# Gated linear attention and a two-level mixture of experts on one core: keys turned head by head, new costs in the planner, 26 of 48 masks on VectorE instead of 21

## The chip, the cores and the metric

The kernel runs on one core of a Trainium2 chip. The core has five engines that run side by side, each through its own list of instructions in order: TensorE (PE in the rows; its weight loads are PEld), VectorE (DVE), ScalarE (ACT), GpSimd (POOL) and SyncE (SP, which here only issues transfers). Sixteen DMA engines move the data. The metric is device time in microseconds (us), lower is better. The kernel before took 367.25 us (median of 3 runs, 365.06 to 367.86).

## The reference, cut to what matters

```
# attention: B=4 batches, H=8 heads, S=768 steps, D=48 wide, all float32
for t in range(S):
    state = alpha[:, :, t, :, None] * state + einsum('bhd,bhe->bhde', k[:, :, t], v[:, :, t])
    y[:, :, t] = einsum('bhd,bhde->bhe', q[:, :, t], state)
x = y.transpose(0, 2, 1, 3).reshape(3072, 384)          # B*S tokens, H*D wide
# mixture of experts: 4 groups of 4 experts, one expert per token, F=1024
g_logits = x @ w_group; g_idx = argmax; g_w = softmax at g_idx
e_logits = x[g] @ w_expert[g]; e_idx = argmax; e_w = softmax at e_idx
out[token] = g_w * e_w * (relu(x @ w1[g, e]) @ w2[g, e])
```

## The kernel before, in words

**Attention.** The 768 steps of a batch are cut into 6 chunks of 128 steps, which makes 24 chunks, numbered 0 to 23; three batches end with chunks 5, 11 and 17, the last with 23. The heads lie in pairs on the partitions: head 2p on rows 0 to 47, head 2p+1 on rows 64 to 111. For each chunk, in the order in which data moves on:

- SyncE loads the chunk (`load`, L486: 962.5 KB with decays, keys, queries and values). Six homes in SBUF are used in turn, and four chunks borrow the homes of the experts' weights. Between the loads of chunks 8 and 12 four transfers fill the experts' slots with zeros (`fill`, L838, 1372 KB each).
- VectorE makes products of the decays with two scans: `back` (L494, backwards), a reciprocal (L500), `forth` (L505).
- GpSimd multiplies them into the keys (`keys`, L510) and the queries (`queries`, L514).
- TensorE makes the scores (`scores`, L528), in two banks, `zs0` and `zs1`, one for each head of a pair; turns the keys (`turned_keys`, L557: four transposes, each of a pair of heads, 112 rows by 128 columns in, 112 columns of identity streamed); makes the key-value products (`gains`, L570), the own outputs from masked scores (`outputs`, L594), the outputs from the state before (`from_before`, L603), and turns the finished rows back (`to_rows`, L617), which gives the routing logits too.
- A mask is due on each of the two score banks. Either VectorE makes it with one multiplication (`mask_all`, L537), or ScalarE copies the bank (`mask_copy`, L542) and GpSimd cuts the copy (`mask_cut`, L545). The table `BY_VECTOR` (L814) says for each chunk how many of the two VectorE takes.
- ScalarE copies the turned keys (`kept_keys`, L562) and the outputs (`copied`, L609), scales the state (`scaled`, L583); VectorE adds the gain to it (`grown`, L579). Chunks 5, 11, 17 and 23 need no turned keys and no gain.

When the logits of a group of chunks are there (6 chunks each in batches 0 to 2; 3, 2 and 1 chunks in the last), VectorE chooses each token's expert in a row of some 13 small operations (L683 to L722), TensorE counts (`counts`, L791), VectorE turns the counts into places, and GpSimd sends the rows of each chunk to their expert's slots (`scatter`, L769, 24 in all).

**Early expert work.** While the last chunks finish, TensorE already computes 96 rows of expert 0 (`add_hidden`, `add_result`, L306) out of batches 0 and 1. After the last scatter has landed, SyncE and ScalarE fetch the rows of the expert that is ahead in count (`fetch_fixed`, L823), VectorE transposes them (`columns_fixed`, L831), and the first full expert can start.

**Experts.** Some 228 us of matrix products follow, expert by expert (`seven`, L1222).

**What sets the order.** For all of the attention, a planner in the kernel's own code (`Plan`, L28) writes the order of every engine's list before anything runs. Each step has an engine, an assumed time `us`, and the steps it comes after; `LAG` is the assumed time from one engine's end to another's start. `order` (L52) takes, again and again, the engine that can start soonest and on it the ready step with the longest way still ahead. A random spread of up to 0.5 us each way, drawn from `seed`, breaks the balance between near equals. TensorE's steps, SyncE's transfers and the scatters are each chained in a fixed sequence of their own (`row=`), so the planner moves freely only the steps of VectorE, ScalarE and GpSimd. At run time each list is kept strictly: a step that waits holds up whatever stands behind it on its engine.

The first eight transfers are issued by SyncE and ScalarE in turn (`begin`, L874).

Of the kernel before, what the change touches and what calls it, by code (L numbers as in the profile page):

```python
# [23 lines left out]
P = 128  # L24
# [3 lines left out]
class Plan:  # L28

    LAG = {ENG.PE: 0.2, ENG.DVE: 0.1, ENG.Activation: 0.2, ENG.Pool: 0.12, ENG.SP: 0.1}  # L30
# [4 lines left out]
    def add(self, name, eng, us, fn, after=(), row=None, lands=0.0, lead=0.0,  # L35
# [8 lines left out]
        return name  # L44

# [6 lines left out]
    def order(self, patience, seed=0, spread=0.0):  # L52
# [28 lines left out]
        while len(done) < len(ops):  # L81
# [12 lines left out]
            free[e] = start + ops[n]["us"]  # L94
            at[n] = start
            done.append(n)
            for m in nexts[n]:
                early[m] = max(early[m], free[e] + self.edge(n, m))
                waits[m] -= 1
                if not waits[m]:  # L100
                    ready[ops[m]["eng"]].append(m)
# [9 lines left out]
def gla_then_hierarchical_moe(  # L111
# [292 lines left out]
    with ExitStack() as gla:  # L404
# [149 lines left out]
        def turned_keys(c):  # L554
            c.zt = output_banks(chunks[max(c.n - 1, 0)])[:, :, 2 * P:2 * P + 2 * R]
            for p in range(HP):
                nc.tensor.transpose(c.zt[:, p // 2, p % 2 * R:(p % 2 + 1) * R], c.k[:, p, :],  # L557
                                    ident[0:R, 0:R])

        def kept_keys(c):  # L560
            c.kt = work.tile([P, HP * R], F32, name="kt")
            nc.scalar.copy(out=c.kt.rearrange("s (b r) -> s b r", b=2), in_=c.zt)  # L562

        def gains(c):
            z = bank()
            for p in range(HP):
                for i in range(2):
                    h = 2 * p + i
                    r = slice(64 * i, 64 if i == 0 else R)
                    nc.tensor.matmul(z[r, p * D:(p + 1) * D],  # L570
                                     lhsT=c.kt[:, p * R + r.start:p * R + r.stop],
# [242 lines left out]
        BY_VECTOR = [1, 0, 0, 1, 1, 2, 0, 0, 0, 1, 1, 2, 1, 1, 1, 0, 0, 2, 2, 1, 0, 2, 0, 2]  # L814
# [51 lines left out]
        L = 400.0  # L866
# [5 lines left out]
        add("first_byte", SP, 1.9, lambda: None, row="sp")  # L872

        def begin(name, by_act, n, a=0, b=IW):  # L874
            add(name, SP, (b - a) * P * 4 / 383.0 / 1e3,
                partial(load, chunks[n], a, b, nc.scalar if by_act else nc.sync),
                row="sp", lands=0.3)
# [3 lines left out]
        begin("decay0", False, 0, 0, HW)  # L881
        begin("decay_0", True, 0, HW, AW)
        begin("key_0", False, 0, AW, KQ)
        begin("query_0", True, 0, KQ, VW)
        begin("decay1", False, 1, 0, AW)
        begin("key_1", True, 1, AW, KQ)
        begin("query_1", False, 1, KQ, VW)
        begin("decay2", True, 2, 0, AW)
# [86 lines left out]
        def add_turned(n):  # L975
# [3 lines left out]
            PEQ(f"turn_k{n}", 0.52, partial(turned_keys, c),  # L979
                after=["ident", late(n - 2, "copy"), late(n - 1, "kept")]  # L980
                + ends_of(n, "key", c.back))
            add(f"kept{n}", ACT, 0.54, partial(kept_keys, c),
# [737 lines left out]
```

## Time and profile before

| what | value |
|---|---|
| median of 3 runs | 367.25 us (365.06 to 367.86) |
| the profiled execution | 367.92 us, of which the span of the trace is 366.2 us |
| TensorE busy in the span | 353.6 us (97%) |
| VectorE busy | 293.1 us (80%) |
| GpSimd busy | 212.8 us (58%) |
| ScalarE busy | 182.0 us (50%) |
| attention with the early expert work | 0 to 128.5 us |
| experts | 128.5 to 356 us |
| last deliveries | 356 to 366.2 us |
| DMA | 98.87 MB, mean 270 GB/s |

Busy shares over the whole span say little here: the kernel is a chain of stages, and which engine or transfer ends last differs from stage to stage. The chain of waits, read from the last instruction back, says what each stretch hangs on, and the timeline of one engine with its idle times says how much room it had. Matmul ends in the trace are modelled, so the start of the next block is the better measure of how long a block took.

### The profile page before, as it was taken

What the parts mean: (1) busy time and instruction counts of PE and PEld (TensorE: products, weight loads), DVE (VectorE), ACT (ScalarE), POOL (GpSimd) and SP (SyncE); (2) the same over time, 40 slices, a digit from 0 to 9 for tenths busy, and PEclk for the clock granted to TensorE, in tenths of its full rate; (3) what the DMA queues carried; (4) which work ended last, traced back from release to release, by engine and by line L of the source; (5) the groups of instructions that cost most, each with busy time, mean ns of one, the idle gap of its engine ahead of it and who ended that gap; (6) DMA issues with size and microseconds to landing.
All of it is one profiled execution on the core that took longest, in us unless ns stands there. A gap on an engine that the chain in (4) does not pass through costs nothing.

```text
span 366.2 us, 16766 instructions
## 1 busy us (share of the span) xinstructions
PE 353.6 (97%) x6890; PEld 331.6 (91%) x6890; DVE 293.1 (80%) x660; ACT 182.0 (50%) x523; POOL 212.8 (58%) x240
## 2 busy tenths in 40 slices
PE   7899999999999999999999999999999999999994
PEld 5688877888888999999999999999999999999994
DVE  6789679999977878989898998988988988895010
ACT  2566755685664142534544445454554454453340
POOL 6898948999986221353544646446354444454544
PEclk9999999999999999999999999999999999999999
DMA  7999997878989599988878878878988988788101
GB/s 271 386 405 384 373 400 287 304 249 300 370 281 401 142 348 238 305 325 235 238 256 231 257 255 254 270 220 286 268 234 281 269 250 302 257 276 274 60 20 35
DMA packets 42461, 98.87 MB, mean 270 GB/s; under 512 B 18853, under 2 KB 23075, under 8 KB 42384
## 3 DMA queue, kind: packets, MB, share of 16 engines
q1 hardware_dynamic: 36496, 87.14, 72.2%
q0 software_dynamic: 4832, 9.55, 7.4%
q8 instruction: 55, 0.90, 1.0%
q10 hardware_dynamic: 1056, 1.10, 0.9%
q14 instruction: 22, 0.18, 0.1%
HBM read 82.61 MB, written 15.60 MB: 268 GB/s over the span
## 4 chain that ended last, share of the span: by engine, by line
PE 80%; DMA 6%; POOL 5%; DVE 4%; issue 3%; ACT 1%; POOLq 0%; SPq 0%; DVEq 0%
PE bank L1222 55%; PE bank L306 5%; DMA ws<-in_rows_dram 5%; PE bank L617 4%; PE zs L528 4%; PE zo L594 3%; PE zs L306 3%; PE zo L603 2%; PE bank L570 2%; PE zo L557 2%; DMA in<-in_rows_dram 2%; DVE kd L494 1%; POOL ws L514 1%; POOL sm L545 1%; DVE ws L287 1%
## 5 line engine op out<-in xcount | busy, mean ns | idle before, releaser
L1370 POOL DMA_INDIRECT out_dram<-yq,dst_q x101 | 109.4, 1083 | 129.3 <-ACT yq L1368 100.9
L1222 PE MATMUL bank<-ts,ws 128*64 128x108 f32 (+13 forms) x1344 | 64.2, 247 | 0.3 <-issue 0.3
L1222 PEld LDWEIGHTS bank<-ts,ws 128*64 128x64 f32 x1344 | 60.2, 137 | 1.0 <-issue 0.4
L1222 PE MATMUL bank<-hT,w 128*64 128x108 f32 (+27 forms) x896 | 58.7, 288 | 0.1
L1222 PEld LDWEIGHTS bank<-hT,w 128*64 128x64 f32 x896 | 50.7, 137 | 4.3 <-ACT hT L1259 0.3
L1222 PE MATMUL bank<-xt_e,w 128*64 128x106 f32 (+12 forms) x1040 | 50.3, 247 | 0.0
L1222 PEld LDWEIGHTS bank<-xt_e,w 128*64 128x64 f32 x1040 | 46.0, 137 | 0.0
L1259 ACT ACTIVATE hT<-hT 128x432 f32<-128x432 f32 (+13 forms) x56 | 29.1, 530 | 21.8 <-DVE hT L1288 15.9
L287 DVE TENSOR_TENSOR ws<-w 128x512 f32<-128x512 f32 x56 | 38.3, 684 | 0.0
L1222 PE MATMUL bank<-ts,w 128*64 128x108 f32 (+13 forms) x672 | 33.2, 247 | 0.0
L1368 ACT ACTIVATE yq<-yq,xq 128x96 f32<-128x96 f32 x91 | 33.0, 373 | 0.3 <-DMA out_dram<-yq,dst_q 0.3
L1222 PEld LDWEIGHTS bank<-ts,w 128*64 128x64 f32 x672 | 30.1, 137 | 0.0
L1363 DVE STREAM_TRANSPOSE yq<-yT 128x672 f32<-128x672 f32 (+2 forms) x16 | 12.9, 809 | 19.8 <-ACT yT L332 12.6
L771 POOL DMA_INDIRECT slots_d<-xr,place x24 | 24.1, 1005 | 5.7 <-issue 4.1
L617 PE MATMUL bank<-wr,yt 112*64 112x116 f32 x384 | 25.4, 267 | 1.0 <-DVE sums L579 0.7
L617 PEld LDWEIGHTS bank<-wr,yt 112*64 112x64 f32 x384 | 20.3, 137 | 1.7 <-issue 0.8
L1326 ACT COPY yT<-bank 128x216 f32<-128x216 f32 (+13 forms) x14 | 4.5, 323 | 34.7 <-PE bank L1222 34.7
L583 ACT ACTIVATE state<-sums,kd 112x48 f32<-112x48 f32 x64 | 17.9, 331 | 6.9 <-DVE sums L579 6.2
L542 ACT COPY sm<-zs 128x512 f32<-128x512 f32 x27 | 15.5, 588 | 10.2 <-PE zs L528 8.9
L609 ACT COPY yt<-zo 112x512 f32<-112x512 f32 x24 | 14.0, 582 | 12.5 <-PE zo L603 10.4
L287 DVE TENSOR_TENSOR ws<-ws,w 128x512 f32<-128x512 f32 x28 | 19.4, 692 | 1.0
L287 DVE TENSOR_TENSOR ws<-w,ws 128x512 f32<-128x512 f32 x28 | 18.7, 668 | 0.0
(221 smaller groups left out, 712.7 us busy)
## 6 DMA issues: line engine op xcount, KB each, us to landing
w<-in_w_dram SPq DMA_DIRECT2D x84, 512.0 KB
ws<-in_rows_dram SPq DMA_DIRECT2D x11, 962.5 KB
w<-in_w_dram SPq DMA_DIRECT2D x6, 1536.0 KB
in<-in_rows_dram SPq DMA_DIRECT2D x6, 962.5 KB
slots_d<-blank SPq DMA_DIRECT2D x4, 1372.0 KB
w<-in_rows_dram SPq DMA_DIRECT2D x4, 962.5 KB
xq<-slots_d SPq DMA_DIRECT2D x28, 85.8 KB
xq<-slots_d SPq DMA_DIRECT2D x28, 73.5 KB
```

Of the source, the lines that this page charges most:

```text
L287: nc.vector.tensor_tensor(out=out, in0=in0, in1=in1, op=op)
L306: nc.tensor.matmul(z, lhsT=w, rhs=x, start=first, stop=last, skip_group_check=True)
L528: nc.tensor.matmul(c.zs[i][s, p, :], lhsT=c.k[r, p, s], rhs=c.q[r, p, :], start=True, stop=True)
L542: nc.scalar.copy(out=c.sm[:, i], in_=c.zs[i])
L583: nc.scalar.activation(out=c.st[:, p, 0:D], in_=chunks[c.n - 1].sums[:, p], func=AF.Copy, scale=c.kd[:, p, 0:1])
L609: nc.scalar.copy(out=c.yt.rearrange("r (a b) s -> r b a s", b=2), in_=c.zo[0:R, :, 0:2 * P].rearrange("r b (a s) -> r b a s", a=2))
L617: nc.tensor.matmul(z[s, p * W:(p + 1) * W], lhsT=c.yt[:, p, s], rhs=wr[:, p, :], start=True, stop=True)
L771: sent = nc.gpsimd.indirect_dma_start(out=slots_by[t], out_offset=bass.IndirectOffsetOnAxis(ap=m["place"][:, c:c + 1], axis=0), in_=xr[:, ...
L1222: nc.tensor.matmul(z[h], lhsT=w[:, h], rhs=x, start=start, stop=False, skip_group_check=True)
L1259: A.activation(out=c, in_=c if z is None else z, func=AF.Relu)
L1368: nc.scalar.activation(out=yq[:, b, :], in_=yq[:, b, :], func=AF.Copy, scale=rows[:, b, QW - 2:QW - 1])
L1370: nc.gpsimd.indirect_dma_start(out=out_by.popleft().rearrange("n (j w) -> (n j) w", j=4), out_offset=bass.IndirectOffsetOnAxis(ap=dst[:, b ...
```

## The change

Five things change. (1) The planner's costs: `LAG` for VectorE and ScalarE are smaller, a step now blocks its engine for a little less than its results take (`OVER`, `held`), some steps' times and the assumed bandwidth `L` are new, and the seed is another. (2) The keys are turned with eight transposes of one head each, on rows 0 to 47 and 64 to 111 by turns, with 48 columns streamed each; the two heads of a pair write to two different banks. (3) The copy of the turned keys is 384 columns wide and not 448, and `gains` reads its weights where they now lie. (4) Among the first transfers, the decays of chunk 1 (now by ScalarE) and the queries of chunk 0 (now by SyncE) swap places. (5) `BY_VECTOR` gives VectorE 7, 2, 6 and 11 masks in batches 0 to 3, and before 5, 4, 6 and 6.

```diff
-    LAG = {ENG.PE: 0.2, ENG.DVE: 0.1, ENG.Activation: 0.2, ENG.Pool: 0.12, ENG.SP: 0.1}
+    LAG = {ENG.PE: 0.2, ENG.DVE: 0.08, ENG.Activation: 0.1, ENG.Pool: 0.12, ENG.SP: 0.1}
+    OVER = {ENG.PE: 0.0, ENG.DVE: 0.09, ENG.Activation: 0.11, ENG.Pool: 0.07, ENG.SP: 0.0}
+    def held(self, o):
+        return o["us"] - min(self.OVER[o["eng"]], 0.4 * o["us"])
...
-            free[e] = start + ops[n]["us"]
+            free[e] = start + self.held(ops[n])
...
-                early[m] = max(early[m], free[e] + self.edge(n, m))
+                early[m] = max(early[m], start + ops[n]["us"] + self.edge(n, m))
...
-            c.zt = output_banks(chunks[max(c.n - 1, 0)])[:, :, 2 * P:2 * P + 2 * R]
+            c.zt = output_banks(chunks[max(c.n - 1, 0)])[:, :, 2 * P:2 * P + HP * D]
             for p in range(HP):
-                nc.tensor.transpose(c.zt[:, p // 2, p % 2 * R:(p % 2 + 1) * R], c.k[:, p, :],
-                                    ident[0:R, 0:R])
+                for i, r in enumerate(heads):
+                    nc.tensor.transpose(c.zt[:, i, p * D:(p + 1) * D], c.k[r, p, :],
+                                        ident[r, r])
...
-            c.kt = work.tile([P, HP * R], F32, name="kt")
-            nc.scalar.copy(out=c.kt.rearrange("s (b r) -> s b r", b=2), in_=c.zt)
+            c.kt = work.tile([P, 2 * HP * D], F32, name="kt")
+            nc.scalar.copy(out=c.kt.rearrange("s (i r) -> s i r", i=2), in_=c.zt)
...
+                    k0 = (i * HP + p) * D
...
-                                     lhsT=c.kt[:, p * R + r.start:p * R + r.stop],
+                                     lhsT=c.kt[:, k0:k0 + r.stop - r.start],
...
-        BY_VECTOR = [1, 0, 0, 1, 1, 2, 0, 0, 0, 1, 1, 2, 1, 1, 1, 0, 0, 2, 2, 1, 0, 2, 0, 2]
+        BY_VECTOR = [1, 1, 1, 1, 2, 1, 0, 0, 0, 0, 1, 1, 1, 2, 1, 0, 0, 2, 2, 2, 1, 2, 2, 2]
...
-        L = 400.0
+        L = 392.0
...
-        add("first_byte", SP, 1.9, lambda: None, row="sp")
+        PAIRS = (("decay0", "decay_0"), ("key_0", "decay1"), ("query_0", "key_1"),
+                 ("query_1", "decay2"))
+        add("first_byte", SP, 2.26, lambda: None, row="sp")
...
-        begin("key_0", False, 0, AW, KQ)
-        begin("query_0", True, 0, KQ, VW)
-        begin("decay1", False, 1, 0, AW)
-        begin("key_1", True, 1, AW, KQ)
...
+        for pair, late_by in zip(PAIRS, (0.3, 0.4, 1.1, 1.1)):
+            us = sum(spans[x][2] - spans[x][1] for x in pair) * P * 4 / 345e3 / 2
+            for i, name in enumerate(pair):
+                begin(name, i == 1, *spans[name], us=us, lands=late_by + (0 if i else us))
...
-            PEQ(f"turn_k{n}", 0.52, partial(turned_keys, c),
+            PEQ(f"turn_k{n}", 0.33, partial(turned_keys, c),
...
-        plan.emit(patience=0.2, seed=5, spread=1.0)
+        plan.emit(patience=0.2, seed=0, spread=1.0)
```

TensorE's list keeps its order of blocks; only the four transposes of a chunk become eight. What the planner moves shows at three places.

**VectorE, around the scan back of chunk 12** (`kd<-ws_884` before, `kd<-ws_956` now; `sums` is the state grown by chunk 10 in the first of these rows, `sm` a mask). Before:

```order
L537 TENSOR_TENSOR sm<-zs_910,causal 128x512
L494 SCALAR_TENSOR_TENSOR kd<-ws_884,starts 112x516
L500 RECIPROCAL starts<-kd 112x4
L505 SCALAR_TENSOR_TENSOR cq<-ws_884,starts 112x516
L579 TENSOR_TENSOR sums<-state_120,bank 112x192
L494 SCALAR_TENSOR_TENSOR kd<-ws_927,starts 112x516
```

and now:

```order
L541 TENSOR_TENSOR sm<-zs_945,causal 128x512
L585 TENSOR_TENSOR sums<-state_120,bank 112x192
L498 SCALAR_TENSOR_TENSOR kd<-ws_956,starts 112x516
L504 RECIPROCAL starts<-kd 112x4
L509 SCALAR_TENSOR_TENSOR cq<-ws_956,starts 112x516
L541 TENSOR_TENSOR sm<-zs_1028,causal 128x512
L498 SCALAR_TENSOR_TENSOR kd<-ws_1011,starts 112x516
L585 TENSOR_TENSOR sums<-state_119,bank 112x192
```

The growth of chunk 10's state stood behind both scans of chunk 12 and now stands ahead of them.

**GpSimd, at the keys and queries of chunk 12** (`ws_884` before, `ws_956` now; `slots_d` are scatters). Before:

```order
L771 DMA slots_d<-xr,place 49152x392
L545 AFFINE_SELECT sm<-sm 128x512
L771 DMA slots_d<-xr,place 49152x392
L514 TENSOR_TENSOR ws_884<-ws_884,cq 112x512
L510 TENSOR_TENSOR ws_884<-ws_884,kd 112x512
```

and now:

```order
L777 DMA slots_d<-xr,place 49152x392 x2
L514 TENSOR_TENSOR ws_956<-ws_956,kd 112x512
L518 TENSOR_TENSOR ws_956<-ws_956,cq 112x512
L777 DMA slots_d<-xr,place 49152x392
L549 AFFINE_SELECT sm<-sm 128x512
```

The keys, which need the first scan alone, now come ahead of the queries, which need the second.

**VectorE, behind the last scan** (`cq<-in`, chunk 23; `xt_0` are the early expert's rows, `lg` the logits of chunks 18 to 20). Before:

```order
L505 SCALAR_TENSOR_TENSOR cq<-in,starts 112x516
L353 SCALAR_TENSOR_TENSOR starts<-seen,starts 128x15
...
L362 TENSOR_REDUCE ahead_i<-starts 128x1
L831 STREAM_TRANSPOSE xt_0_91<-rows_0_90 128x3x3x32
L579 TENSOR_TENSOR sums<-state_120,bank 112x192
L637 TENSOR_REDUCE lg<-lgp 128x60
```

and now:

```order
L509 SCALAR_TENSOR_TENSOR cq<-in,starts 112x516
L357 SCALAR_TENSOR_TENSOR starts<-seen,starts 128x15
...
L366 TENSOR_REDUCE ahead_i<-starts 128x1
L541 TENSOR_TENSOR sm<-zs_1999,causal 128x512
L541 TENSOR_TENSOR sm<-zs_1998,causal 128x512
L585 TENSOR_TENSOR sums<-state_120,bank 112x192
L643 TENSOR_REDUCE lg<-lgp 128x60
```

Both masks of chunk 22, which ScalarE and GpSimd made before, now stand here, and the transpose of the early rows has moved some 20 places further back, ahead of the places of chunks 18 to 20.

## Rows read from the trace of the kernel before

**Rows 1.** Stretches: length, busy us (instructions) of each engine; PEclk, DMA share, GB/s.

```profile
5.00:55.00 50.00, 46.35 (x815) 39.72 (x812) 40.28 (x68) 30.42 (x86) 40.77 (x65) 1.00 1.03 387
60.00:105.00 45.00, 44.58 (x994) 38.43 (x986) 42.68 (x85) 30.78 (x91) 42.05 (x43) 1.00 0.86 305
105.00:110.00 5.00, 5.00 (x127) 4.58 (x127) 2.76 (x12) 3.46 (x11) 4.65 (x6) 1.00 0.68 200
128.50:356.00 227.50, 226.74 (x4625) 221.55 (x4626) 184.81 (x424) 106.89 (x306) 105.75 (x98) 1.00 0.80 250
```

**Rows 2.** The chain of waits: start us, us, what.

```profile
37.16 17.31 DMA ws<-in_rows_dram
...
57.19 0.34 DVE sums L579
...
65.13 0.53 PE zo L557 x4
65.66 0.54 PE bank L570 x13
```

**Rows 3.** VectorE's timeline: start us, us, operation, tiles, shapes [idle before <-releaser].

```profile
7.33 1.23 DVE L494 TENSOR_TENSOR_SCAN kd<-in,starts 112x516 f32<-112x516 f32 x1 [1.08 <-DMA in<-in_rows_dram]
...
54.49 1.23 DVE L494 TENSOR_TENSOR_SCAN kd<-ws,starts 112x516 f32<-112x516 f32 x1 [1.51 <-DMA ws<-in_rows_dram]
...
100.00 1.27 DVE L537 TENSOR_TENSOR sm<-zs,causal 128x512 f32<-128x512 f32 x2
...
102.85 1.23 DVE L505 TENSOR_TENSOR_SCAN cq<-in,starts 112x516 f32<-112x516 f32 x1
...
107.07 0.48 DVE L831 STREAM_TRANSPOSE xt<-rows 128x288 f32<-128x288 f32 x1 [2.00 <-DMA rows<-slots_d]
...
111.01 0.68 DVE L537 TENSOR_TENSOR sm<-zs,causal 128x512 f32<-128x512 f32 x1
...
112.60 0.20 DVE L752 TENSOR_REDUCE place<-own 128x3 int32<-128x48 f32 x1
```

**Rows 4.** TensorE's timeline: shapes are rows*columns of the weights, then the streamed operand.

```profile
50.69 1.16 PE L528 MATMUL zs<-in 48*128 48x128 f32 x16 [0.68 <-POOL sm L545]
...
55.19 1.16 PE L528 MATMUL zs<-in 48*128 48x128 f32 x16
56.28 0.67 PE L570 MATMUL bank<-in,kt 128*64 128x48 f32 x16
57.66 1.01 PE L617 MATMUL bank<-wr,yt 112*64 112x116 f32 x16 [0.72 <-DVE sums L579]
...
60.09 1.11 PE L528 MATMUL zs<-ws 48*64 48x128 f32 x32
...
107.79 1.20 PE L528 MATMUL zs<-in 48*64 48x128 f32 x32
...
128.51 1.70 PE L1222 MATMUL bank<-xt_ahead,w 128*64 128x108 f32 x32 [0.68 <-ACT yT L332]
```

**Rows 5.** VectorE's timeline at the start of the first full expert.

```profile
127.53 0.88 DVE L831 STREAM_TRANSPOSE xt_ahead<-rows_ahead 128x672 f32<-128x672 f32 x1 [1.09 <-DMA rows_ahead<-slots_d]
```

**Rows 6.** GpSimd's timeline, same columns as VectorE's.

```profile
57.36 1.18 POOL L514 TENSOR_TENSOR ws<-ws,cq 112x512 f32<-112x512 f32 x1 [0.98 <-DVE cq L505]
58.50 1.18 POOL L510 TENSOR_TENSOR ws<-ws,kd 112x512 f32<-112x512 f32 x1
...
104.17 1.17 POOL L514 TENSOR_TENSOR in<-in,cq 112x512 f32<-112x512 f32 x1 [0.41 <-DVE cq L505]
...
113.70 0.98 POOL L771 DMA_INDIRECT slots_d<-xr,place  x1 [0.30 <-issue]
...
120.86 0.98 POOL L771 DMA_INDIRECT slots_d<-xr,place  x1 [0.16 <-DVE key L374]
```

**Rows 7.** Weight loads by shape, 14 to 116 us: busy us, mean ns, idle before.

```profile
L557 PEld LDWEIGHTS zo<-ident,ws 112*128 112x128 f32 x44 | 4.3, 140 | 1.8 <-ACT yt L609 0.7 <-issue 0.3 <-ACT state L583 0.2
L528 PEld LDWEIGHTS zs<-w 48*128 48x128 f32 x64 | 4.1, 187 | 0.7 <-issue 0.7
```

More of the change, by code (lines that the diff above doesn't have):

```diff
@@ L870, in dma, with begin @@
             add(name, SP, max(us, bytes_ / L / 1e3), fn, after=list(after), row="sp", lands=lands)
-        add("first_byte", SP, 1.9, lambda: None, row="sp")
-        def begin(name, by_act, n, a=0, b=IW):
-            add(name, SP, (b - a) * P * 4 / 383.0 / 1e3,
+        PAIRS = (("decay0", "decay_0"), ("key_0", "decay1"), ("query_0", "key_1"),
+                 ("query_1", "decay2"))
+        add("first_byte", SP, 2.26, lambda: None, row="sp")
+        def begin(name, by_act, n, a=0, b=IW, us=None, lands=0.3):
+            add(name, SP, us or (b - a) * P * 4 / 383.0 / 1e3,
                 partial(load, chunks[n], a, b, nc.scalar if by_act else nc.sync),
-                row="sp", lands=0.3)
+                row="sp", lands=lands)
         KQ, VW = AW + KW, AW + 2 * KW
         HW = HP // 2 * A1 + 1
-        begin("decay0", False, 0, 0, HW)
-        begin("decay_0", True, 0, HW, AW)
-        begin("key_0", False, 0, AW, KQ)
-        begin("query_0", True, 0, KQ, VW)
-        begin("decay1", False, 1, 0, AW)
-        begin("key_1", True, 1, AW, KQ)
-        begin("query_1", False, 1, KQ, VW)
-        begin("decay2", True, 2, 0, AW)
+        spans = dict(decay0=(0, 0, HW), decay_0=(0, HW, AW), key_0=(0, AW, KQ),
+                     query_0=(0, KQ, VW), decay1=(1, 0, AW), key_1=(1, AW, KQ),
+                     query_1=(1, KQ, VW), decay2=(2, 0, AW))
+        for pair, late_by in zip(PAIRS, (0.3, 0.4, 1.1, 1.1)):
+            us = sum(spans[x][2] - spans[x][1] for x in pair) * P * 4 / 345e3 / 2
+            for i, name in enumerate(pair):
+                begin(name, i == 1, *spans[name], us=us, lands=late_by + (0 if i else us))
         begin("value0", False, 0, VW, IW)
@@ L978, in add_turned @@
                 return
-            PEQ(f"turn_k{n}", 0.52, partial(turned_keys, c),
+            PEQ(f"turn_k{n}", 0.33, partial(turned_keys, c),
                 after=["ident", late(n - 2, "copy"), late(n - 1, "kept")]
                 + ends_of(n, "key", c.back))
-            add(f"kept{n}", ACT, 0.54, partial(kept_keys, c),
+            add(f"kept{n}", ACT, 0.48, partial(kept_keys, c),
                 after=[f"turn_k{n}", late(n - 2, "gain")])
@@ L986, in add_rows @@
             c = chunks[n]
-            PEQ(f"row{n}", 0.87, partial(to_rows, c), after=[f"copy{n}", "wr"],
+            PEQ(f"row{n}", 0.83, partial(to_rows, c), after=[f"copy{n}", "wr"],
                 reader=f"logit{n}")
@@ L1015, in add_outputs @@
             c = chunks[n]
-            PEQ(f"own_out{n}", 0.99, partial(outputs, c),
+            PEQ(f"own_out{n}", 1.02, partial(outputs, c),
                 after=[made["masked", n, 0], made["masked", n, 1], late(n - 1, "copy"),
```

## The prediction, made before the changed kernel was run

> **What bounds the kernel now.** I read the stretches first, then the chain of waits, then the timelines of the engines that the chain names.
>
> The stretches split the run in three [rows 1]. From 128.5 us on the experts keep TensorE busy for 226.7 of 227.5 us; the change leaves their code and order alone, so this part is taken as fixed, and so are the 10 us behind it. From 5 to 55 us the DMA share is 1.03: the transfers are full. From 60 to 105 us three engines are nearly full at once: TensorE 44.6 of 45 us, VectorE 42.7, GpSimd 42.1. VectorE's missing 2.3 us lie between 85 instructions, 27 ns each, so it has no room there either. Only from 105 to 110 us does it stand idle for 2.2 of 5 us.
>
> The chain of waits joins the first two stretches at one transfer: the load of chunk 12, issued at 37.16 and landed 17.3 us later, at 54.47 [rows 2]. VectorE stood idle for 1.51 us until it came and began the scan back of chunk 12 at 54.49 [rows 3]. The transfers' bytes and their order from the ninth on are the same in the changed kernel, and they were full from 5 us on, so I take **54.5 us as pinned**: what TensorE saves ahead of it buys nothing by itself.
>
> At the far end, the first full expert starts at 128.51 us [rows 4]. The row puts its wait down to ScalarE, but the transpose of its fetched tokens began at 127.53, took 0.88, had waited 1.09 us for the fetch, and ended just then [rows 5]. The fetch follows the last scatter, which began at 120.86 [rows 6]. So the start of the experts hangs on the chain of scatters, not on TensorE.
>
> **The change, part by part.**
>
> *Masks and order on VectorE, chunks 12 to 23.* Before, VectorE went from the scan of chunk 12 at 54.49 to the end of the last scan, 102.85 + 1.23 = 104.08 [rows 3]: 49.6 us. By the two lists there are now 14 masks in between for 12, and 7 additions of the state's growth for 8 (chunk 10's now stands ahead of the stretch); the rest is the same. Two masks took 1.27 [rows 3], one addition 0.34 [rows 2]: +0.93. The last scan then ends at 54.5 + 49.6 + 0.9 = **105.0 us**, 0.9 later than before. GpSimd began chunk 23's queries 0.09 behind the scan and took 1.17 [rows 6], and chunk 23's keys now stand ahead of its queries: its scores can start at 105.0 + 0.1 + 1.2 = **106.3 us**, where they started at 107.79 before [rows 4]: 1.5 us gained, though VectorE itself is later.
>
> *TensorE in the same stretch.* Before, GpSimd made chunk 12's queries first, until 57.36 + 1.18 = 58.54, and then the keys, until 59.68 [rows 6]; the scores started at 60.09 [rows 4]. With the keys first, the scores can start at 58.6. From there to chunk 23's scores TensorE took 107.79 − 60.09 = 47.7 us. Even with no cheaper transpose it gets there at 58.6 + 47.7 = 106.3, as VectorE allows.
>
> *The transposes.* Today a chunk's four take 0.53 us [rows 2]. No row shows the new form. From below: `gains` streams 48 columns too, in 16 recorded passes that run as 8 pairs, in 0.54 [rows 2]; the new form has four pairs, 0.27. From above, if a pair takes as long as one transpose today, 0.53; if the two row halves did not run side by side, 1.06. I take 0.36, near `gains`, since the number of columns is the same: 0.17 saved in each. Ten of them lie between chunk 12's scores and chunk 23's: 1.7 us, which TensorE then spends waiting for VectorE (104.6 against 106.3). I put them at nothing there; the cover is VectorE's list, and if it were 1.7 us shorter the saving would show.
>
> The row that speaks for pairs side by side is that of the scores before chunk 12: weights of 48 rows by 128 columns, on the two row halves by turns, load for 187 ns each (those of today's transposes for 140) [rows 7], 16 times in a block that took 56.28 − 55.19 = 1.09 us [rows 4]. One after the other the loads would need 3.0 us. Against the change speaks the Trainium skill, "TensorE: Matmul & The Clock Gate", section "LDWEIGHTS (loading the stationary operand)": a load costs by its columns, not by its rows, some 107 ns for 128 of them. By that rule alone eight loads would need 0.85 us (an estimate from the page) for half as much today. The same page's section "The mechanism" lets loads pass running products on other row groups, and with that the trace agrees. The rule gives the second rival.
>
> *The copy of the keys* is a seventh narrower, on ScalarE, which is busy for 30.8 of 45 us: nothing. *The first transfers*: chunk 1's scan had waited 1.08 us for its decays at 7.33 [rows 3]; they now come earlier and chunk 0's queries later. Between nothing and 1.1 us gained, all of it ahead of the pinned load: nothing in the sum.
>
> *The end of attention.* Behind the last scan the wait of 2.00 us for the early rows and their transpose of 0.48 move away, and chunk 22's two masks, 1.27, move in [rows 3]. Chunk 23's second mask ended at 111.01 + 0.68 = 111.69; now at 111.7 + 0.9 − 2.5 + 1.3 = 111.4, soon enough for a TensorE that is 1.5 us earlier. The places of chunks 18 to 20 stood at 112.80 [rows 3]; they come 0.3 sooner with the masks but stand behind the transpose of 0.48 now: 113.0. Chunk 18's scatter began at 113.70 [rows 6], so it gains at most 0.6: 113.1. Scatters follow each other by 0.98 + 0.30 = 1.28 us [rows 6], and 113.1 + 5 × 1.28 = 119.5, with two small touches in between 119.6, against 120.86 for the last one. The experts start **1.2 us sooner**, at 127.3; TensorE's own 1.5 us don't all arrive.
>
> *Sum:* −1.2 us. The profiled execution took 367.92 (span 366.2, 1.7 around it), so 366.7 by that execution, which lies 0.67 above the median of 367.25. Against the median: 367.25 − 1.2 = **366.1 us**.
>
> **The rivals.**
>
> *1. VectorE's new order makes it wait (slower).* Chunk 10's growth now stands ahead of chunk 12's first scan. It needs `gains` of chunk 10, which ran from 56.28 to some 56.95, with the addition at 57.19 [rows 2, 4]. If TensorE is no sooner there, chunk 12's scan begins at 57.3 and not 54.5. The last scan then ends at 107.8, the scores of 23 start at 109.1, chunk 18's scatter at 115.9, the last at 122.3 for 120.86: +1.4, **368.7 us**. It decides from the point where `gains` of chunk 10 ends after 54.2, less than 2.7 us sooner than today. For enough speed: eight transposes (chunks 2 to 4 and 6 to 10) at 0.17 give 1.4, the wait of 0.68 for a mask's cut at 50.69 may go [rows 4], and the first transfers give up to 1.1, 3.2 in all. One of the three missing is enough for part of the loss. Chance 0.20, for half of the price or more.
>
> *2. The row halves don't run side by side (much slower).* Then a chunk's transposes take 1.06. Ahead of chunk 12 that is 8 × 0.53 = 4.2 us; its scan waits behind chunk 10's growth until 61.5, its scores start at 65.6, and with ten more times 0.53 chunk 23's start at 118.6, +10.8: **378 us**. The scores' loads [rows 4, 7] speak against it. Chance 0.04.
>
> *3. VectorE gives more than counted.* If it could keep pace with TensorE, chunk 23's scores would start at 104.6 and the experts some 3 us sooner: **364.2 us**. It would need 1.7 us out of a list whose only gaps are 27 ns long. Chance 0.06.
>
> *4. Nothing arrives.* GpSimd, too, is 93% full from 60 to 105 us; if chunk 23's queries or the places of 18 to 20 slip by another us, the scatters start as before: **367.2 us**. Chance 0.12.
>
> **How the numbers follow.** The forecast, 0.5 to 2.0 us sooner, has 0.58; alone it spans 365.2 to 366.8. The three runs before lay 2.8 us apart, which widens it by some 0.5 each way for a median. Eight in ten: from 364.4, which takes in most of rival 3, to 368.4, which takes in rival 4 and most of rival 1. About 1%, 3.7 us, is what can be told from no change: below 363.6 only the far end of rival 3, 0.05; above 370.9 rival 2 and an accident beyond rival 1, 0.06; within, 0.89.
>
> **What would show it.** Right: the scan of chunk 12 still begins at 54.5 behind a DMA; chunk 12's scores at about 58.6; the last scan ends near 105.0, later than before, and chunk 23's scores start near 106.3; the transposes take 0.3 to 0.4; TensorE now shows waits of 1 to 2 us in all between 60 and 105 us, which it had not; the last scatter begins near 119.6 and the first full expert near 127.3. Wrong: chunk 12's scan behind an addition instead of a DMA (rival 1), transposes of over 0.53 (rival 2), a load of chunk 12 that lands at another time, or an expert stage that is not 227.5 us long, which would mean that the change reaches where I took it to be fixed.

## The result: slower by 0.75%, and the profile after

The changed kernel took **369.7 us** (median of 20 runs, 367.4 to 374.1) against 367.1 for the kernel before (20 runs, 365.1 to 370.6): ratio **1.0075**, 95% interval 1.0054 to 1.0096. The forecast was 366.1 with a range of 364.4 to 368.4: wrong in sign and outside its range, though less than 1% from no change, as the largest of its chances said.

The profiled execution took 368.16 us (span 366.5). It is one of the quickest of the changed kernel (below: the quick profile), while the 367.92 of the profile before lay above its median, so the two traces show less than the whole loss. Where medians and ratios differ a little below, it is because the ratios leave out disturbed executions.

The attention did almost what was predicted. VectorE's timeline, GpSimd's, then TensorE's (start us, us, operation, [idle before <-releaser]), to be read beside [rows 3, 4, 6]:

```profile
53.78 1.23 DVE L498 TENSOR_TENSOR_SCAN kd<-ws,starts 112x516 f32<-112x516 f32 x1 [1.62 <-DMA ws<-in_rows_dram]
...
102.36 1.23 DVE L509 TENSOR_TENSOR_SCAN cq<-in,starts 112x516 f32<-112x516 f32 x1
```

```profile
112.18 0.97 POOL L777 DMA_INDIRECT slots_d<-xr,place  x1 [0.30 <-issue]
...
119.28 0.98 POOL L777 DMA_INDIRECT slots_d<-xr,place  x1 [0.16 <-DVE key L376]
```

```profile
57.87 1.10 PE L532 MATMUL zs<-ws 48*64 48x128 f32 x29 [0.30 <-POOL ws L518]
59.91 0.43 PE L532 MATMUL zs<-ws 48*64 48x128 f32 x3 [0.94 <-issue]
60.28 0.45 PE L562 MATMUL zo<-ident,ws 48*128 48x48 f32 x8
60.66 1.01 PE L623 MATMUL bank<-wr,yt 112*64 112x116 f32 x16
...
98.33 0.32 PE L562 MATMUL zo<-ident,ws 48*128 48x48 f32 x4 [0.33 <-issue]
...
104.34 0.91 PE L623 MATMUL bank<-wr,yt 112*64 112x116 f32 x13 [0.74 <-issue]
...
106.52 1.07 PE L532 MATMUL zs<-in 48*64 48x128 f32 x32
...
129.19 2.44 PE L1229 MATMUL bank<-xt_ahead,w 128*64 128x108 f32 x48 [2.92 <-issue]
```

The eight transposes take 60.66 − 60.28 = 0.38 us; chunk 23's scores start at 106.52; the last scatter begins at 119.28, 1.58 us sooner than before. But the first full expert starts at 129.19, **0.68 later** than before, after TensorE had stood idle for 2.92 us. Its row says "issue", yet VectorE's transpose of that expert's rows ended only at 128.21 + 0.88 = 129.09, and it had waited for their fetch:

```profile
128.21 0.88 DVE L837 STREAM_TRANSPOSE xt_ahead<-rows_ahead 128x672 f32<-128x672 f32 x1 [3.31 <-DMA rows_ahead<-slots_d]
```

What lies between shows in the queue of SyncE (SPq), of the kernel before and then of the changed one (`rows` are the early rows, `w` the weights of the expert that is ahead, `rows_ahead` that expert's rows):

```profile
100.87 2.34 SPq L823 DMA_DIRECT2D rows<-slots_d  x4
105.80 0.41 SPq L258 DMA_DIRECT2D w<-in_w_dram  x1
106.39 0.42 SPq L264 DMA_DIRECT2D w<-in_w_dram  x1
124.09 0.89 SPq L823 DMA_DIRECT2D rows_ahead<-slots_d  x2
```

```profile
104.49 2.69 SPq L829 DMA_DIRECT2D rows<-slots_d  x4
108.24 0.41 SPq L262 DMA_DIRECT2D w<-in_w_dram  x1
108.84 0.39 SPq L268 DMA_DIRECT2D w<-in_w_dram  x1
124.59 0.90 SPq L829 DMA_DIRECT2D rows_ahead<-slots_d  x2
```

The fetch of the early rows goes 3.6 us later, though scatter 11, the last that it needs, began at the same time (94.36 and 94.23); so 3.1 MB of weights go 2.4 us later. The DMA queues show what that does: q0 is the scatters' data, q1 what SyncE issued (packets, MB, share of 16 engines). Before, from 110 to 117 and from 118 to 122 us:

```profile
q1 hardware_dynamic: 547, 2.16, 77.3%
q0 software_dynamic: 203, 0.65, 23.3%
...
q0 software_dynamic: 273, 0.83, 54.9%
q1 hardware_dynamic: 7, 0.02, 1.3%
```

and after:

```profile
q1 hardware_dynamic: 576, 2.29, 92.1%
q0 software_dynamic: 64, 0.22, 7.7%
...
q0 software_dynamic: 316, 0.97, 61.4%
q1 hardware_dynamic: 150, 0.55, 33.8%
```

Scatters that were issued sooner deliver a third of the data in the first stretch, and share the second with the weights' tail. From the last scatter's begin to SyncE's fetch of `rows_ahead` it is 124.59 − 119.28 = 5.3 us, where it was 124.09 − 120.86 = 3.2.

**Why the fetch waits.** All its rows lie in one DRAM buffer, `slots_d`. Written into the program, a fetch waits for every scatter written ahead of it; the kernel exempts the early fetch (`declare_no_dep`) only from scatters written behind it. The new planner's order puts scatter 12 ahead of the fetch. Each engine's list is the same either way; the built programs differ in one number, the fetch's wait on the semaphore that scatters 4 and 12 share: 32 for 16. It now waits for 13 scatters.

### The profile page after: what moved, and what is told of

The parts are those of the page before. It is cut to its first block, busy times and chain, and to the rows that moved or that the text cites. A ratio compares the mean times of both kernels' runs of the same rounds, so it can differ in the third digit from the quotient of the medians.

```text
span 366.5 us, 16915 instructions
## 1 busy us (share of the span) xinstructions
PE 349.1 (95%) x6970; PEld 331.0 (90%) x6970; DVE 296.0 (81%) x665; ACT 178.7 (49%) x518; POOL 209.1 (57%) x235
## 4 chain that ended last, share of the span: by engine, by line
PE 72%; DVE 10%; DMA 9%; issue 4%; POOL 3%; ACT 1%; SPq 0%; POOLq 0%; DVEq 0%; ACTq 0%
PE bank L1229 55%; PE bank L310 5%; DMA slots_d<-blank 4%; PE zs L310 3%; DMA ws<-in_rows_dram 3%; DVE kd L498 3%; DVE cq L509 2%; PE bank L623 2%; PE zs L532 2%; PE zo L600 2%; DMA in<-in_rows_dram 2%; DVE sm L541 1%; PE zo L609 1%; PE bank L576 1%; DVE ws L291 1%
## 5 line engine op out<-in xcount | busy, mean ns | idle before, releaser
L1229 PEld LDWEIGHTS bank<-hT,w 128*64 128x64 f32 x896 | 51.9, 137 | 3.1 <-ACT hT L1266 0.3
L623 PE MATMUL bank<-wr,yt 112*64 112x116 f32 x384 | 25.6, 267 | 1.2 <-issue 0.7
L623 PEld LDWEIGHTS bank<-wr,yt 112*64 112x64 f32 x384 | 20.3, 137 | 2.0 <-issue 1.0
L546 ACT COPY sm<-zs 128x512 f32<-128x512 f32 x22 | 12.9, 590 | 11.9 <-PE zs L532 11.8
L498 DVE TENSOR_TENSOR_SCAN kd<-ws,starts 112x516 f32<-112x516 f32 x12 | 14.6, 1213 | 3.7 <-DMA ws<-in_rows_dram 3.7
```

Source lines behind the costliest of these rows:

```text
L498: nc.vector.tensor_tensor_scan(out=flat(c.kd[:, p0:p1])[:, ::-1], data0=c.t[0:R, A1 * p1:A1 * p0:-1], data1=one_col.to_broadcast([R, A1 * ...
L546: nc.scalar.copy(out=c.sm[:, i], in_=c.zs[i])
L623: nc.tensor.matmul(z[s, p * W:(p + 1) * W], lhsT=c.yt[:, p, s], rhs=wr[:, p, :], start=True, stop=True)
L1229: nc.tensor.matmul(z[h], lhsT=w[:, h], rhs=x, start=start, stop=False, skip_group_check=True)
```

## Experiments

On two of the four chips used here the kernel before takes 367 us; on the other two it takes about 413, and every kernel run on them takes 412 to 418. Every ratio is against the kernel before on the same chip.

**1. The fetch's wait, taken out and put in.**

```diff
 # fetch_first: the changed kernel; every engine's list stays
+        done.remove("fetch0"); done.insert(done.index("scatter12"), "fetch0")
 # before_fetch_late: the kernel before; every engine's list stays
+        done.remove("fetch0"); done.insert(done.index("scatter12") + 1, "fetch0")
```

> The changed kernel as it is, once more, beside the kernel before on one chip. Both theories: median 369 to 371, above the kernel before by 2 to 3 us; the early rows are fetched (SyncE) at about 104.5, the weights of the expert ahead are issued at about 108.2, the last scatter begins at 119.3, the first full expert at 129.2. If the clock theory holds, its executions show a granted clock below 1.0 in most, and the time follows it.

> The changed kernel, with the fetch of the early rows written ahead of scatter 12 again, as in the kernel before: every engine's list stays, only the fetch waits for 12 scatters and not 13. Theory 1 (the fetch's one more scatter holds SyncE, the weights of the expert ahead come late and stand in the last scatters' way): the fetch goes at about 101 (104.5), the weights at 105.3 (108.2), the rows of the expert ahead are fetched at about 122.4 (124.5), the first full expert starts at about 127.0 (129.2), TensorE stands idle under 1 us ahead of it (2.9); profiled time about 366.0, median 366 to 367.5. Theory 2 (the attention's new order itself costs the time, whatever the fetch does): the first full expert stays at 129 and the median at 369.7.

> The kernel before, with the fetch of the early rows written behind scatter 12, as in the changed kernel: every engine's list stays, only the fetch waits for 13 scatters and not 12. Theory 1: scatter 12 began at 100.36 and lands at about 104.6, so the fetch goes at about 105 (100.9), the weights of the expert ahead at 108.8 (105.8), the rows of the expert ahead at 125 to 126 (124.0), the first full expert at 129.5 to 130.5 (128.5): 1 to 2 us slower than the kernel before, 368.1 to 369.1. Theory 2: no change, 367.1.

On one chip (kernel before 366.78): the changed kernel 372.59, ratio 1.0118 (1.0071 to 1.0165); with the fetch ahead 367.39, **1.0003** (0.9966 to 1.0040); the kernel before with the fetch behind 370.43, **1.0121** (1.0079 to 1.0164). One wait in the program makes and unmakes the loss. The queue of SyncE with the fetch ahead, and TensorE's first full expert:

```profile
100.37 2.61 SPq L829 DMA_DIRECT2D rows<-slots_d  x4
104.88 0.41 SPq L262 DMA_DIRECT2D w<-in_w_dram  x1
105.48 1.35 SPq L268 DMA_DIRECT2D w<-in_w_dram  x1
122.50 0.90 SPq L829 DMA_DIRECT2D rows_ahead<-slots_d  x2
```

```profile
126.91 2.44 PE L1229 MATMUL bank<-xt_ahead,w 128*64 128x108 f32 x48 [0.88 <-ACT yT L336]
```

Each of these starts is within 0.7 us of what was expected. In the kernel before, the late fetch costs by another road, which I had not foreseen: there VectorE transposes the early rows ahead of masks and choices, so it waits, then ScalarE for VectorE, then TensorE for ScalarE; the first full expert starts at 131.15 (expected 129.5 to 130.5), and the time is 370.43 for the 368.1 to 369.1 expected. From the last scatter to the fetch of the rows ahead it is 3.2 us here, as before, so this run speaks for the wait and not for the weights. VectorE, then TensorE:

```profile
108.82 0.48 DVE L831 STREAM_TRANSPOSE xt<-rows 128x288 f32<-128x288 f32 x1 [4.89 <-DMA rows<-slots_d]
```

```profile
110.65 1.81 PE L617 MATMUL bank<-wr,yt 112*64 112x116 f32 x16 [2.20 <-ACT yt L609]
```

Behind that wait TensorE's granted clock was 0.56 and 0.58 from 110 to 112 and from 112 to 114 us, which adds to the loss. This edit also lets two of TensorE's banks change places in some blocks of the built program, and two of its waits with them; at the row shown the wait that ended last is still that for ScalarE.

The changed kernel itself came out slower than expected here (369 to 371): its early fetch goes at 108.05, its first full expert starts at 132.26. Part 3 says what else happened in that execution.

> The changed kernel once more beside these: 369 to 371.5, 0.6 to 1.2% above the kernel before; a third profile of it. The early fetch at 104 to 108 us and the rows of the expert ahead at 124.5 us or later, where the same order with the fetch ahead of scatter 12 had 100.4 to 101.8 and 122.5 to 124.3.

On a 413 us chip: 414.14, 1.0012 (0.9978 to 1.0046). There the loss does not show: the last scatter begins at 127.33, and its rows are fetched 3.2 us later, though the early fetch is late (106.65).

**2. The weights in the scatters' way.**

```diff
 # after_w21_behind: the changed kernel, the early fetch as late as in it
+        done.remove("w21"); done.insert(done.index("fetch1") + 1, "w21")
 # fetch_first_w21: both edits
```

> The changed kernel, the early fetch as late as in it (104.5 us), but the second-layer weights of the expert ahead issued by SyncE behind its share of the fetch of that expert's rows: 1.5 MB less stand in front of the last scatters' data. Theory 1's link (the weights stand in the scatters' way): the last scatter begins at 119.3 as before and its rows are fetched at 122.0 to 122.8 (124.5), the first full expert starts at about 127 (129.2), median 367 to 368. If the late fetch costs in another way: rows fetched at 124.5, first full expert at 129, median 369.7 to 371.

> Once more, because the chip of the run before took 413 us for the kernel before, too, and its last scatters waited for other things. The early fetch as late as in the changed kernel (about 104.5 us), the second-layer weights of the expert ahead issued behind its rows' fetch. Theory 1's link (the weights stand in the last scatters' way): the last scatter begins at 119.3, the rows are fetched at 122.0 to 122.8 (124.5), first full expert at about 127 (129.2), median 1 to 2 us below the changed kernel's 369.7. Otherwise: 124.5 and 129, no gain.

`w21` is the second-layer weights of the expert ahead, `fetch1` SyncE's share of the fetch of its rows. The first run, on a 413 us chip, gave 417.86, 1.0102 (1.0065 to 1.0139): slower than the changed kernel was on such a chip, by a cause that its one profile, from the quickest of ten executions, does not show. The second, on a chip of 367: 367.78, **1.0018** (0.9995 to 1.0041). GpSimd's last scatter and SyncE's queue:

```profile
120.22 0.98 POOL L777 DMA_INDIRECT slots_d<-xr,place  x1 [0.16 <-DVE key L376]
```

```profile
106.04 2.72 SPq L829 DMA_DIRECT2D rows<-slots_d  x4
109.54 0.41 SPq L262 DMA_DIRECT2D w<-in_w_dram  x1
123.09 1.24 SPq L829 DMA_DIRECT2D rows_ahead<-slots_d  x2
124.54 0.40 SPq L268 DMA_DIRECT2D w<-in_w_dram  x1
```

The early fetch goes still later (106.04), and the rows behind it are up to 1.1 us later than expected, with the first full expert at 128.07 for about 127. Yet with half the weights in front the rows are fetched 2.9 us after the last scatter began, not 5.3, and the time falls by as much as expected. The link is shown for chips of 367 us: in the changed kernel the late fetch costs by way of the weights.

> The changed kernel with both: the early fetch ahead of scatter 12, and the second-layer weights of the expert ahead behind its rows' fetch. Theory 1: the rows are fetched at about 121.8 (122.5 with the first alone), but TensorE's early expert work ends at 126.1 either way, so the first full expert starts at 126.5 to 126.9: no more than 0.4 us below the first alone, 366.5 to 367.4; at the bottom of that it is as fast as the kernel before or 0.5 us faster.

368.04, 1.0041 (1.0010 to 1.0073): above the 366.5 to 367.4 expected, and no better than the first edit alone. The rows come at 121.88 and the first full expert at 126.73, as expected, but the weights moved behind are late in turn: VectorE waited for them, then TensorE for ScalarE.

```profile
133.12 0.69 DVE L291 TENSOR_TENSOR ws<-w 128x512 f32<-128x512 f32 x1 [3.23 <-DMA w<-in_w_dram]
```

```profile
137.42 3.88 PE L1229 MATMUL bank<-hT,w 128*64 128x216 f32 x48 [1.39 <-ACT hT L1266]
```

**3. Is it the idle TensorE itself?**

```diff
         plan.emit(patience=0.2, seed=0, spread=1.0)
+        warm(20)
```

> The changed kernel with 20 products of constants (bf16, 256 columns) on TensorE behind the early expert work, so that its 2.9 us without work ahead of the first full expert are filled for about 2.3 us. Theory 3 (the idle time itself lowers TensorE's granted clock in the expert stage, which makes the rest of the loss and the spread): the first full expert stays at 129.2, the granted clock is 1.0 in nearly all executions, the median falls to 368.0. Theory 1 alone, without the clock: no change, 369 to 370.

369.8, 1.0071 (1.0046 to 1.0095): what the changed kernel had at first (1.0075), but 2.8 us below after_again beside it on the same chip (1.0118; the two intervals overlap). In the profile the products fill 2.35 us, the first full expert starts at 130.00, and the clock stays at 1.00. So the late fetch keeps its price when the idle time is filled; whether the filling saves something in other executions is open, and the next profile shows that it can.

The profile of after_again, 373.1 us, shows what an idle TensorE can cost in an unlucky execution. The load of chunk 10 came 2.0 us later than in the quick profile (VectorE's scan at 42.76 for 40.77), TensorE waited 2.32 us, and its granted clock then fell from 2.4 to 1.2 GHz, to a mean of 0.67 and 0.65 of full speed in two stretches. It fell again behind the 2.75 us ahead of the first full expert, the third stretch (length, busy us of the engines, clock, DMA share, GB/s):

```profile
45.00:50.00 5.00, 3.07 (x42) 2.98 (x44) 4.49 (x16) 3.00 (x9) 2.12 (x5) 0.67 1.05 389
50.00:55.00 5.00, 5.00 (x67) 4.23 (x64) 3.21 (x6) 2.27 (x8) 3.53 (x3) 0.65 1.02 413
130.00:135.00 5.00, 2.74 (x31) 2.77 (x33) 2.65 (x9) 0.79 (x2) 0.00 (x0) 0.70 0.89 219
```

```profile
46.93 0.66 PE L562 MATMUL zo<-ident,w 48*128 48x48 f32 x8 [2.32 <-ACT yt L615]
...
132.26 3.97 PE L1229 MATMUL bank<-xt_ahead,w 128*64 128x108 f32 x48 [2.75 <-issue]
```

```profile
54.08 0.26 DVE L751 TENSOR_TENSOR own<-bank,picked 128x96 f32<-128x96 f32 x1 [1.24 <-ACT seen L747]
...
55.03 0.69 DVE L541 TENSOR_TENSOR sm<-zs,causal 128x512 f32<-128x512 f32 x1 [0.41 <-PE zs L532]
55.81 0.35 DVE L585 TENSOR_TENSOR sums<-state,bank 112x192 f32<-112x192 f32 x1
56.08 1.22 DVE L498 TENSOR_TENSOR_SCAN kd<-ws,starts 112x516 f32<-112x516 f32 x1
```

In the quick profile the block at 46.93 had waited 0.35. VectorE's rows show what follows: chunk 12's scan starts straight behind the growth of chunk 10 and not behind its load, 2.3 us later than in the quick profile. The growth itself did not wait; VectorE had waited 1.24 us for the counts and 0.41 for scores, both late from TensorE's slow stretch. The first full expert starts 3.1 us later than in the quick profile, and its first block of products takes 3.8 us up to the next block's start for 2.2. The two make 4.6 of the 4.9 us between the spans. How many executions go this way is not known. The mean clock over all executions was 0.990 with the change (20 runs) and 0.997 before (23 runs); what of the loss it carries was not separated.

**4. The new transposes alone, and the new order without them.** The three functions `turned_keys`, `kept_keys` and `gains` are exchanged, and nothing else (the edit is shortened here).

```diff
 # before_new_keys: the kernel before        # fetch_first_old_keys: fetch_first
-    transpose(zt[pair], k[:, p], ident[0:R, 0:R])   # 4 of 112 rows
+    transpose(zt[i], k[r, p], ident[r, r])          # 8 of 48 rows; the other way round there
```

> The kernel before with only the keys' part of the change: eight transposes of one head each, the copy 384 wide, the gains' weights where they now lie; all lists else as before. The sum of the prediction: a chunk's transposes take 0.38 us for 0.53, and the 20 times 0.15 us are hidden by the load of chunk 12 and by VectorE's list: no change, 366.5 to 367.5. Clock theory (what TensorE saves turns into waits in front of late transfers, in which its granted clock falls): 368 to 370, mean clocks near 0.990 as in the changed kernel. If TensorE is the bound after all: 365 to 366.

> Once more, on another chip: the kernel before with the new transposes alone. The prediction's sum: no change, 366.5 to 367.5. If the new transposes' instructions make TensorE's stops: 1 us and more of them between 55 and 128 us, and 0.5 to 1.5 us slower than the kernel before.

> A third time, since the first two were on chips that take 413 us for the kernel before: the kernel before with the new transposes alone. The prediction's sum: no change, ratio 0.998 to 1.002, and the transposes 0.38 us for 0.53 a chunk. If the new transposes cost through instruction supply: stops of TensorE of 1 us and more between 55 and 128 us, ratio 1.002 to 1.005.

> The changed kernel with the early fetch ahead of scatter 12, and with the old transposes (four a chunk, of 112 rows and 112 columns) in the new order. Clock theory: TensorE has less to wait for, mean clocks rise from 0.994 to 0.997, and it is faster than the same kernel with the new transposes (367.4): 366 to 366.8. If the new transposes earn what they save behind chunk 12: 10 times 0.15 us less about 1.1 us of waits that are there, 0.4 us slower, 367.8.

> Once more, on another chip: early fetch ahead of scatter 12, the new order, the old transposes (4 products a chunk for 8). If the additional instructions of the new transposes make the stops of TensorE (1.5 to 2.9 us between 55 and 128 us in the changed order, 0 to 0.4 in the old order with the old keys): stops under 0.6 us and 366 to 366.8. If the order makes them: stops of 1 us and more as with the new keys, and 367 to 368.

> A third time for the same reason: early fetch ahead of scatter 12, the new order, the old transposes. If the new transposes hold the new order back: stops under 0.6 us, 366 to 366.8. If they do not: stops of 1 us and more as with the new transposes, 367 to 368.

All six fell on 413 us chips. The new transposes alone: 0.9987 (0.9958 to 1.0015), 1.0016 (0.9980 to 1.0051), 0.9992 (0.9960 to 1.0024): no change, as the sum had it. The new order with the old transposes: 1.0019 (0.9982 to 1.0057), 1.0030 (0.9995 to 1.0064), 1.0041 (1.0004 to 1.0077): not faster either. TensorE's stops between 55 and 128 us came to 0.6 to 2.6 us in the first three profiles and to 1.7 to 1.9 in the others: the transposes do not decide them. Whether the same holds where the kernel takes 367 was not measured.

**5. Where the rest of the gain goes.**

```diff
 # fetch_first_light, in load_part: leaves out 2 of 3 parts of second-layer weights
         weights[i] = weights[i - 2]
+        if layer and c != 1: return
```

> The changed kernel with the early fetch ahead of scatter 12, once more beside the others: 366.5 to 367.5, within 0.4% of the kernel before; a second profile. If its lead over the kernel before at the first full expert is again 1.5 to 2.6 us and again shrinks behind 270 us, the expert stage gives back; if it was a single execution's accident, the lead stays.

> The changed kernel with the early fetch ahead of scatter 12, which from the fourth expert on leaves out two of the three parts of each second-layer weight load (a third of an expert's bytes). In the kernel with all loads the lead of 2.56 us that it had over the kernel before at 271 us fell to 1.23 at 316 us and to 0.65 at the end. Theory W (the weights' transfers set the pace once TensorE is ahead): the lead stays, the last expert work ends 2.3 to 2.6 us sooner than before, 364.8 to 365.8 in all. Other theory (the lead is lost to something else): no change, 367 to 367.8.

> Once more for the same reason: early fetch ahead of scatter 12, from the fourth expert on two of the three parts of each second-layer weight load left out (a third of an expert's bytes). Theory W (the weights' transfers take back the lead that TensorE has): the lead over the kernel before at the first full expert is kept to the end, 1 us or more faster than the same kernel with all its loads. Other theory: the same time as with all loads.

fetch_first again: 367.55, 1.0019 (0.9991 to 1.0046). In its first profile TensorE led the kernel before by 1.6 us at the first full expert and by 2.56 at one of ScalarE's activations between an expert's two layers (268.76 for 271.33), but by 1.23 near the end (328.31 for 329.54), and the span was only 0.6 shorter. The lead shrinks in three steps of 0.4 to 0.5 us, and each falls on a pause of TensorE: at 268.99, too short for the profile to mark, and at

```profile
308.36 1.85 PE L1229 MATMUL bank<-xt_e,w 128*64 128x90 f32 x42 [0.29 <-issue]
...
313.68 0.76 PE L1229 MATMUL bank<-xt_e,w 128*64 128x90 f32 x13 [0.22 <-issue]
```

At each TensorE goes on 1.3 to 1.4 us after a packet of its instructions has landed, as in part 6. In its second profile the first full expert started at 128.92, since TensorE had stopped for 2.9 us between 55 and 128 us with nothing to wait for. The light kernel kept a lead of 2.27 us to the last activation in its profile on a chip of 367, but its times, 413.9 (1.0005; 0.9976 to 1.0034) and 366.65 (0.9998; 0.9962 to 1.0034), do not tell it from the full one: theory W is not shown. The changed kernel's profile has none of these pauses either, with all its loads.

**6. The stops.** In the profiles of the changed order TensorE stops, marked "issue" (it waits for nothing that the profile shows), at the same two instructions: in the rows above 98.33 (behind four of eight transposes) and 104.34 (behind three of sixteen products). Of the eleven such profiles with the new transposes all have the second and six the first, none of these on a 413 us chip. after_w21_behind_2 has them at

```profile
98.45 0.32 PE L562 MATMUL zo<-ident,ws 48*128 48x48 f32 x4 [0.60 <-issue]
...
105.28 0.91 PE L623 MATMUL bank<-wr,yt 112*64 112x116 f32 x13 [1.56 <-issue]
```

```diff
 # fetch_first_shift: 16 more products at the start; the planner's cost for them unchanged
-        PEQ("warm1", 0.115 * WARM[1], partial(warm, WARM[1]))
+        PEQ("warm1", 0.115 * WARM[1], partial(warm, WARM[1] + 16))
```

> The changed kernel with the early fetch ahead of scatter 12, and 16 more products of constants on TensorE at the very start (32 instructions). In five profiles of the changed order TensorE stops, with nothing to wait for, at the same two instructions: in the middle of chunk 22's eight transposes (at 98 us) and behind the third product of the block that turns chunk 21's rows back (at 104 us), 127 products apart. Theory F (it waits for its instructions, which come in packets of 16,384 bytes, 256 instructions): the stops move by 16 products, to the last third of chunk 22's scores and into the gains of chunk 22; size 0.3 to 1.6 us as before, time the same, 366.5 to 368. Other theory (something in those blocks): the stops stay where they are.

414.33, 1.0032 (1.0002 to 1.0063), on a 413 us chip. A stop now stands exactly 16 products ahead of the first place, 12 before the end of the 32 scores; the second, behind the third product of L623, is gone:

```profile
100.37 0.77 PE L532 MATMUL zs<-ws 48*64 48x128 f32 x12 [1.54 <-issue]
```

So a stop belongs to a place in the instruction stream, not to the work there. The queue that brings the instructions moves 56 packets, 0.92 MB, in the changed kernel's profile, 16,384 bytes each:

```profile
q8 instruction: 56, 0.92, 1.0%
```

The Trainium skill, "Runtime: NRT & Kernel Launch", section "Instruction fetch mechanics", says that instructions come in blocks of 16 KiB, 256 instructions, and that crossing a boundary is mostly hidden. The trace agrees with both: the 127 products between the two stops, each with its weight load, make 254 instructions, and the built program has two more between them that only wait; and of 11 block ends between 57 and 128 us in the changed kernel's profile eight show no stop. The other three cost 2.0 us in all.

Two more readings fit. Counted through the built programs, all 21 stops between 55 and 128 us in the profiles on chips of 367 us lie whole multiples of 256 instructions apart, the two of the kernel before among themselves; one is off by one instruction. And in five of these profiles TensorE goes on, at each of 14 stops, 1.3 to 1.6 us after a packet has landed (in the changed kernel's at 98.33 after 96.96, and at 104.34 after 102.82). Why those packets come late is not shown. The DMA share was 1.0 in the stop ahead of 98.33, but it fell to 0.02 in that ahead of 104.34, and lay at 0.1 to 0.3 in the longest, 1.56 us.

## Why the prediction was wrong, point by point

- *The load of chunk 12 as a pinned point:* held in the quick profile, 53.78 for the 54.5 forecast, and in the six others of the new order on chips of 367 us that are like it, 52.6 to 53.9: VectorE still waited for the DMA, and rival 1 (the growth of chunk 10 ahead of the scan) did not decide. In after_again it did not hold: 56.08, behind that growth and with no wait for the load. That is the sign given for rival 1, though VectorE's list was late there for other reasons.
- *Transposes* 0.38 for 0.36: right. The two of a pair start 3 to 4 ns apart in the trace, so the row halves do run side by side, and rival 2 is out.
- *Chunk 12's scores* at 57.87 (58.6), *chunk 23's* at 106.52 (106.3): right in time, half wrong in cause. VectorE's last scan ended at 102.36 + 1.23 = 103.6, not at 105.0; the stretch took 49.8 us where I had summed 50.5, which I did not follow up. (VectorE's masks before were 5, 4, 5 and 7 in the four batches, not 5, 4, 6 and 6 as stated with the change; the sum went by the lists and is not touched.) It was TensorE that came last: GpSimd had chunk 23's queries ready at 105.81, and TensorE had lost 0.94 + 0.33 + 0.74 us in stops and not in waits for VectorE. Without them the scores could have started at some 105.9 (an estimate from that row), so 0.6 us of the saved transposes, put at nothing, would have shown.
- *The scatters:* the last at 119.28 (119.6): right by luck. Chunk 18's began at 112.18 and not at 113.1 (its places were ready at 111.79, not 113.0). From it to the last the sum had 6.5 us, but it took 7.1, and the rows of before had said so: 113.70 to 120.86. With that the forecast would have been 120.3, a gain of 0.6 us.
- **The step that failed is "The experts start 1.2 us sooner, at 127.3".** I carried the scatters' gain over as if the fetch followed the last scatter by a fixed time, 3.2 us in the trace of before. It took 5.3, because the weights' transfer stood 2.4 us later in the same queues. I had read that the transfers' bytes and order were unchanged and took that for unchanged times. The planner did not mean the fetch to be later: it puts it at 95.1 us, where it had 96.3, but it moves scatter 12 from 98.3 to 94.4 and so writes it ahead, and it does not know the wait that this makes. With the wait taken out, the first full expert starts at 126.91 in one profile and at 128.92 in another, with its stops: the step was right but for the wait, and the wait is worth 2.2 of the 3.6 us between forecast and result (369.7 to 367.5).
- *The expert stage as fixed:* true of the changed kernel's profile (129.19 to 356.13 us). But where TensorE came earlier, in fetch_first, it gave back half, at three pauses for instructions; the predicted −1.2 us in the total is not reached even without the wait (1.0003 and 1.0019). Stops in the instruction supply are shown as a part of that, 2.9 us ahead of the experts in the second profile and 1.3 within them in the first; what they make of the median is not settled.
- *The rivals:* none of the four had this mechanism. Nearest in its path was "nothing arrives", 367.2, by a chance of 0.12. Rival 1's sign, a scan of chunk 12 that does not wait for its load, is seen in one execution of the changed kernel; what such executions make of the median was not separated.

No version that was run beats the kernel before; the changed kernel with the fetch written first is level with it.

## What to carry to other kernels

An engine's list tells the order, not the waits: of every transfer that reads a shared DRAM buffer ask which writes stand ahead of it in the program, for it waits for all of them. Before a gain at one step is carried to the next, look at what else is in the DMA queues between the two: a transfer that moves later can take the whole of it. And a saving on an engine that waits for something else is worth nothing there, as the new transposes were on the chips where they were tried alone.

## What the runs showed of the hardware

- TensorE stopped for 0.2 to 1.6 us at some of the 16,384-byte boundaries of its instructions and went on 1.3 to 1.6 us after a packet of instructions had landed, with DMA shares from 0.02 to 1.0 meanwhile. On the 413 us chips there were 16 to 19 stops of about 0.4 us marked "issue" in the expert stage of a profile, on the others up to three.
- The rows of a scatter that took 1.0 us to issue were fetched 3.2 us after its begin with free queues, and 5.3 us behind 3 MB of weights.
- The granted clock fell to 1.2 GHz for some 7 us after TensorE had been idle for 2.3 us, and for some 3.5 us after 2.75 us in the same execution; it did not fall after 2.92 us of idle time in another.
